# Load sizes at the start, one routing pass and item 0's loads rearranged in a fused attention and mixture-of-experts kernel

## The chip, the cores and the metric

The kernel runs on one core of one Trainium2 chip. The metric is the device time of one execution in microseconds (us), from three runs. "Within 0.2%" means within 1.8 us of the time before.

## The reference

Two stages follow each other; the second takes the first one's output as 14592 tokens of 256 channels.

```python
# q, k, v: (4, 3648, 256)
qn = q / (norm(q, axis=1) + 1e-06)
kn = k / (norm(k, axis=1) + 1e-06)
s = kn.transpose(0, 2, 1) @ qn / tau          # (4, 256, 256)
a = softmax(s)
x = (v @ a).reshape(14592, 256)

# 4 groups of 4 experts; each token takes the best group, then its best expert
g_idx = argmax(x @ w_group);  g_w = softmax weight of that group
e_idx = argmax(x @ w_expert[g_idx]);  e_w = softmax weight of that expert
out = g_w * e_w * (relu(x @ w1[g, e]) @ w2[g, e])   # w1: 256x1024, w2: 1024x256
```

## The kernel before, in words

**Precision.** Most matmuls are made of three fast ones: an operand is split into a high part (a copy on ScalarE, ACT) and a low part (a subtraction on VectorE, DVE), and high by high, high by low and low by high are summed in PSUM on TensorE (PE). A few are left as plain float32; the trace records each of those twice.

**Scores.** q and k of a batch come in eight units of four row groups each (`GJ` = 4; the last of a batch is small); unit `u` is one tile `qkraw` of 128 x 2 x 4 x 256, loaded by `s_load(u)` on SyncE's queue (SP). `LOADS` = 4 units are issued ahead, in five buffers. For unit 0 the loads come in three pairs (row group 0; 1; 2 and 3), for unit 1 in two pairs (0 and 1; 2 and 3), and from unit 2 on one pair, q then k. Each partition's run in memory is 1 KB per row group. `s_split(u)` splits row group 3 (in later units others too) and squares the unit on ACT for the norms, `s_mm(u)` does the matmuls (L240): groups 0 to 2 of the first units are plain, 3 is split. Fourteen `wake` matmuls run before the first load is there.

**Rows of x.** `x_load(u)` brings v, `x_tr(u)` transposes it on PE into two PSUM buffers `vtr` (one per half of the channels) and splits it: `vth` on ACT (L326), `vtl` on DVE (L327). `x_mm(u)` (L349) multiplies by the softmax matrix, which has the routing logits folded in as 20 more columns, and calls `hooks[k]` behind the row groups that they name. With `TM` = 30 the loop `for t in range(TM, len(xs_at))` lays down the order of every engine by hand; `k` counts its turns, and k = 0 is unit 20 of x. `adv(n)` runs n steps of the generators in `rgens`, in their order.

**Routing.** `routing(b, j0, j1)` picks group and expert for the rows of a range in eight steps, nearly all on DVE: steps 1 to 3 pick, 4 counts within a partition, 5 sends the counts to PE and computes the weights, 6 adds the carried counts (L437 to L441), 7 makes the slots `si` (L444, L446), 8 puts the row groups into `pend`. `pre_gen` follows it for the table of the first four items (L558 on, `tb_pre`). Batch 2 has the ranges 0 to 8, 8 to 20 and 20 to 29; `PRE` = (2, 20) ends the rows that the first items are drawn from.

**Scatters.** `scatter(n)` writes each row group of a range to its slots in HBM (`x_sorted`) by an indirect DMA on GpSimd (POOL, L473); behind each stands a `pause()`, a fill of 128x256 zeros (L163).

**Experts.** Items of 512 rows of one expert follow each other. `fetch_w` and `fetch_x` put their loads on SP: for item 0, at k = 8, w1 (1 MB), then its rows (which wait until every scatter up to `PRE` has landed), then w2 in two halves. `split_w` and `split_x` make the high and low parts, `ffn1` (L995 to L1005) and `ffn2` (L1036, L1037, L1045) the two products, `send` scatters the output. Leftover rows go in pieces of 32, four at once on four columns of the array ("quads", `q_ffn1` L1155); `q_xT` turns their rows by 32x64 transposes on DVE (L1140), 16 of them per quad in two lots. They stand behind `split_w` of the next item in the loop over (item, f).

The change touches `s_load` (L186), `scatter` (L483), `fetch_w` and `fetch_x` (L724 to L751), `hooks` (L933), the turn k = 8 (L966), and the place of `q_xT` (L1362).

Of the kernel before, what the change touches and what calls it, by code (L numbers as in the profile page):

```python
# [17 lines left out]
P = 128  # L18
B, NT, C = 4, 3648, 256
N = B * NT  # L20
E = 16
FF = 1024
# [3 lines left out]
GPB = 8  # L26
# [4 lines left out]
RW = 272  # L31
# [19 lines left out]
PRE = (2, 20)  # L51
# [14 lines left out]
def attention_moe(ctx: ExitStack, tc, q, k, v, tau, w_group, w_expert, w1, w2, out):  # L66
# [94 lines left out]
    def pause():  # L161

        POOL.memset(zero[:, 0:256], 0.0)  # L163
# [18 lines left out]
    def s_load(u):  # L182
        rows, nj = rows_of(u % GPB)
        raw = spool.tile([P, 2, GJ, C], F32, tag="raw", name="qkraw", bufs=LOADS + 1)

        for j0, j1 in (((0, 1), (1, 2), (2, nj)), ((0, 2), (2, nj)))[u] if u < 2 else ((0, nj),):  # L186
            for i, src in ((0, q), (1, k)):
                SP.dma_start(raw[:rows, i, j0:j1, :], tiles_of(src, u // GPB, u % GPB)[:, j0:j1, :])
        su[u] = dict(raw=raw)
# [269 lines left out]
    def scatter(n, wait=0):  # L459
        for _ in range(n):  # L460
            if not pend or pend[0][1] + wait > now[0]:
                break
            (b, j0), _, j, si = pend.pop(0)
            g, t = divmod(j0 + j, GJ)
            rows, nj = rows_of(g)
            xs = rows_at[b, g]
            if t == 0:
                tok = xs[:, 0:nj, C].bitcast(I32)
                if g < NG:
                    POOL.iota(tok, pattern=[[-1, GJ]], base=NOID - b * NT - g * GJ, channel_multiplier=-J)  # L470
                else:
                    POOL.iota(tok, pattern=[[0, 1]], base=NOID - b * NT - J * P, channel_multiplier=-1)
            ins = POOL.indirect_dma_start(  # L473
                out=xs_d, out_offset=bass.IndirectOffsetOnAxis(ap=si[:rows, j:j + 1], axis=0),
                in_=xs[:rows, t, 0:RW].bitcast(I32), in_offset=None, bounds_check=NSLOT - 1, oob_is_err=False)
            if not before((b, j0)):
                for o in early:
                    tc.declare_no_dep(ins.ins, o, reason="the first items' slots have been filled")
                late.append(ins.ins)
            for o in scatters:  # L480
                tc.declare_no_dep(ins.ins, o, reason="every token has a slot of its own")
            scatters.append(ins.ins)
            pause()  # L483


    def table_steps(items, cnt, start, held, stride, name):
# [233 lines left out]
    def raw_tile(of=3):  # L720
        raw_n.append(0)
        return wp.tile([P, 2048], F32, tag=f"wraw{len(raw_n) % of}", name="wraw", bufs=1)

    def fetch_w(d, tb, i, which):  # L724
        e = SP.value_load(tb[0][0:1, i, 0:1], min_val=0, max_val=E - 1)
        src, n = (w1e, 2) if which == "w1" else (w2e, 8)
        if d is items[KPRE] and which == "w1":
            raw_n.append(0)
        d[which + "r"] = t = raw_tile(3 if any(d is o for o in items[0:KPRE]) else 2).rearrange("p (c f) -> p c f", c=n)
        for c in range(2) if d is items[0] and n == 8 else ():  # L730
            h = slice(c * n // 2, (c + 1) * n // 2)
            SP.dma_start(t[:, h, :], src[ds(e, 1), c * FF // 2:(c + 1) * FF // 2, :].rearrange("o (c p) f -> p (o c) f", p=P))
        if d is not items[0] or n == 2:
            SP.dma_start(t, src[ds(e, 1), :, :].rearrange("o (c p) f -> p (o c) f", p=P))

    def fetch_x(d, tb, i):

        if d is items[0]:
            d["xg"] = raw_tile()[:, 0:4 * RW].rearrange("p (t w) -> p t w", t=4)
        else:  # L740
            d["xg"] = ring(4, RW, name="xg")
        d["nv"] = tb[1][:, i:i + 1]
        if tb is not tb_pre:
            gather(d["xg"].rearrange("p t w -> p (t w)"), tb[2][:, i:i + 1], 4)
            pause()
            return
        s = SP.value_load(tb[0][0:1, i, 1:2], min_val=0, max_val=DUMMY)
        ins = SP.dma_start(d["xg"].bitcast(I32), xs_d[ds(s, BIG), :].rearrange("(p t) w -> p t w", t=4))
        early.append(ins.ins)
        for o in late:  # L750
            tc.declare_no_dep(ins.ins, o, reason="the first items' slots have been filled")  # L751
# [176 lines left out]
    def where(i):  # L928
# [4 lines left out]
    hooks = {  # L933
        0: {1: [sft()], 2: [sft()]},
        1: {0: [adv()], 1: [sft(), adv()], 2: [sft(2), adv()]},
        2: {0: [sft(), adv()], 1: [sft(), lambda: x_tr(US - GPB)], 2: [adv()], 3: [adv()]},
        3: {0: [adv(2)]},
        4: {0: [adv()], 1: [adv()]},
        5: {0: [adv()], 1: [adv()]},
        6: {0: [adv()], 1: [adv()]},  # L940
        7: {0: [adv()], 1: [adv()]},
# [5 lines left out]
    for t in range(TM, len(xs_at)):  # L947
        x = xs_at[t]
        k = t - TM
        now[0] = t  # L950
        if k == 0:
            soft(2)
        if k == 1:
            sp_.close()
            wp = ctx.enter_context(tc.tile_pool(name="wp", bufs=4))
            vx = vx_.enter_context(tc.tile_pool(name="vx", bufs=VX))
            x_load(x + 2)
            x_load(x + 3, vx)
        if k >= 1 and x + 4 < UX:
            x_load(x + 4, vx if x + 4 == UX - 4 else None)  # L960
        if x + 1 < UX and x + 1 != US - GPB:
            x_tr(x + 1, vx if x + 2 == US - GPB else None)
        if k == 0:
            s_mm(US - 2)
            s_mm(US - 1)
        if k == 8:  # L966
            fetch_w(items[0], tb_pre, 0, "w1")
            fetch_x(items[0], tb_pre, 0)
            fetch_w(items[0], tb_pre, 0, "w2")
        if k == 10:  # L970
            vx_.close()
            wb = ctx.enter_context(tc.tile_pool(name="wb", bufs=4))
        if x == UX - 1:
            fetch_x(items[1], tb_pre, 1)
            fetch_w(items[1], tb_pre, 1, "w1")
            split_x(items[0])
            split_w(0, "w2", 0)
        x_mm(x, hooks[k])
        scatter(NJ)
        queue(x)  # L980
# [161 lines left out]
    def q_xT(q, a):  # L1142
        q_turn(qs["xT"][q % 2], qs["xg"][q % 2][:, a * C // 4:(a + 1) * C // 4].rearrange("p (k c) -> p c k", c=2), a)
# [179 lines left out]
    for n in range(len(seq) + lag):  # L1323
# [3 lines left out]
        if n < len(seq):  # L1327
            i, f = seq[n]
            j, jn = host(i), host(i + 1)
            if f == 3:  # L1330
                if KPRE < i + 2 < NBIG:
                    fetch_x(*where(i + 2))
            if jn is not None and f == 5 and i + 2 < NBIG:
                fetch_big(i + 2, "w1")
            for s_, p_ in plan.get((j, f), ()):
                q_weights(s_, p_)
            if f == 7 and KPRE < i + 2 < NBIG:
                quads_of(items[i + 2])
            if j is not None and f == 1 and i + 1 < NBIG:
                fetch_big(i + 1, "w2")  # L1340
            if first(j) is not None and f == 1:
                q = first(j)
                tokens(qs["ids"][q % 2], qs["xg"][q % 2][:, C:C + 1], slotq, tb_pc[1][:, q:q + 1])
            if i == NBIG - 1 and f == 4:
                POOL.drain()
                ns = nc.values_load(nsub[0:1, 0:1], min_val=0, max_val=NSUB)
                tc.mark_branch_hint_location("subs", engines=[ET.PE, ET.Pool, ET.DVE, ET.Activation, ET.SP])
            if first(jn) is not None and f == 1:
                q_rows(first(jn))
            ffn1(items[i], f)  # L1350
            for h in side.get(n, ((), ()))[0]:
                h()
            if KPRE < i + 1 < NBIG:
                if f in (0, 2):
                    split_w(i + 1, "w1", f // 2)
                if f == 3:
                    turn_x(items[i + 1])
                if f == 4:
                    split_x(items[i + 1])
                if f in (5, 6):  # L1360
                    split_w(i + 1, "w2", f - 5)
            for q, a in ((jn, 0),) if f == 7 else ((j, 2),) if f == 0 else ():  # L1362
                if first(q) is not None:
                    q_xT(first(q), a)
                    q_xT(first(q), a + 1)
            if j is not None:
                s_ = stage(j)
                for second, q, hf in q_stage(s_) if s_ is not None else ():
                    if f == 2:
                        (q_ffn2 if second else q_ffn1)(s_, q, hf)  # L1370
                    if 3 <= f < 7 and not second:
                        q_hT(q, hf, f - 3)
                    if f == 3 and second and hf:
                        q_put(q)
# [115 lines left out]
```

## Time and profile before

| | us |
|---|---|
| median of 3 runs | 909.39 |
| the 3 runs | 909.39, 910.15, 909.3 |
| the profiled execution, its own time | 908.52 |
| span of its trace | 906.7 |
| PE busy | 898.0 (99%) |
| DVE busy | 715.2 (79%) |
| ACT busy | 495.1 (55%) |
| POOL busy | 394.1 (43%) |

A trace row gives start and length in us, engine, source line, operation, output<-inputs, shapes and count; in brackets stands how long the engine was idle before it and what ended that. Rows of the same instruction that follow each other are merged (x12). Matmuls are pipelined: a matmul's listed length is longer than its turn, and from start to start is what counts.

### The profile page before, as it was taken

How to read it: one execution, taken by the hardware profiler on the slowest of the kernel's cores; microseconds unless marked ns; L12 is line 12 of the kernel's file. 1: busy time of each engine (PE TensorE's matmuls, PEld its weight loads, DVE VectorE, ACT ScalarE, POOL GpSimd, SP SyncE). 2: the span in 40 equal slices, each digit the busy share in tenths (PEclk: the TensorE clock that was granted, in tenths of full speed). 3: DMA queues.
4: the chain of work that ended last, by engine and by line, in shares of the span. 5: the costliest groups of instructions: out<-in, count | busy, mean ns of one | idle time of the engine just before them, and what ended most of it. 6: DMA issues, size and time to landing. Idle time of an engine off the chain costs nothing. (4 is left out here: it accounts for less than half of the span.)

```text
span 906.7 us, 16702 instructions
## 1 busy us (share of the span) xinstructions
PE 898.0 (99%) x5454; PEld 767.9 (85%) x5454; DVE 715.2 (79%) x1533; ACT 495.1 (55%) x832; POOL 394.1 (43%) x569
## 2 busy tenths in 40 slices
PE   9999999999999999999999999999999999999997
PEld 7899999999899987878787887878787878787887
DVE  6898999977999968888898767787677858786852
ACT  6788788776554444544455444444444444444432
POOL 0001887888588783423332233333433334223223
PEclk9999999999999999999999999999999999999999
DMA  8984868465954476566777778777776667777751
GB/s 301 352 313 163 304 238 298 152 206 183 310 186 167 157 229 213 202 214 232 251 250 251 247 255 260 255 252 238 250 227 227 227 221 236 241 237 255 243 168 39
DMA packets 156075, 209.68 MB, mean 231 GB/s; under 512 B 63025, under 2 KB 115602, under 8 KB 155984
## 3 DMA queue, kind: packets, MB, share of 16 engines
q1 hardware_dynamic: 140928, 164.03, 55.4%
q0 software_dynamic: 15056, 44.54, 13.1%
q8 instruction: 44, 0.72, 0.3%
q14 instruction: 47, 0.39, 0.1%
HBM read 166.14 MB, written 31.17 MB: 218 GB/s over the span
## 5 line engine op out<-in xcount | busy, mean ns | idle before, releaser
L1014 ACT ACTIVATE hh<-hmm 128x512 fp32r<-128x512 f32 (+1 forms) x222 | 131.9, 595 | 337.2 <-PE hmm L1005 279.1
L1005 PE MATMUL hmm<-xth,ww 128*128 128x512 f32 (+1 forms) x888 | 312.3, 392 | 0.0
L1066 POOL DMA_INDIRECT out<-ys,ids x112 | 125.4, 1120 | 356.2 <-DVE ys L1055 331.9
L1036 PE MATMUL wacc<-ww,hh 128*128 128x512 f32 (+1 forms) x736 | 265.6, 394 | 0.0
L1015 DVE SCALAR_TENSOR_TENSOR hl<-hmm,hh 128x512 fp32r<-128x512 f32 (+1 forms) x222 | 151.1, 683 | 110.3 <-ACT hh L1014 91.2
L1037 PE MATMUL wacc<-ww,hl 128*128 128x256 f32 (+1 forms) x736 | 206.2, 280 | 0.0
L1005 PEld LDWEIGHTS hmm<-xth,ww 128*128 128x128 f32 x888 | 166.7, 188 | 36.1
L1005 PE MATMUL hmm<-xtl,ww 128*128 128x512 f32 (+1 forms) x444 | 174.0, 392 | 0.0
L1036 PEld LDWEIGHTS wacc<-ww,hh 128*128 128x128 f32 (+1 forms) x736 | 137.5, 187 | 36.5 <-issue 4.1
L473 POOL DMA_INDIRECT x_sorted<-xs,si x112 | 132.3, 1182 | 58.8 <-issue 26.0
L792 DVE TENSOR_TENSOR ww<-wraw,ww 128x1024 fp32r<-128x1024 f32 x112 | 136.7, 1221 | 19.5 <-ACT ww L791 15.6
L1037 PEld LDWEIGHTS wacc<-ww,hl 128*128 128x128 f32 (+1 forms) x736 | 138.7, 188 | 7.0
L791 ACT ACTIVATE ww<-wraw 128x1024 fp32r<-128x1024 f32 x112 | 117.9, 1053 | 3.9 <-DMA wraw<-in_moe_w 3.8
L1005 PEld LDWEIGHTS hmm<-xtl,ww 128*128 128x128 f32 x444 | 83.8, 189 | 9.6
L163 POOL MEMSET zero<- 128x256 f32 x260 | 87.1, 335 | 0.1
L349 PE MATMUL xmm<-ahi,vth 128*128 128x276 f32 (+1 forms) x232 | 69.1, 302 | 0.6 <-ACT xs L352 0.5
L240 PE MATMUL sacc<-qkraw 128*128 128x256 f32 (+1 forms) x276 | 68.3, 389 | 0.7 <-DMA qkraw<-in_k 0.7
L349 PE MATMUL xmm<-alo,vth 128*128 128x276 f32 (+1 forms) x232 | 67.3, 291 | 0.0
L349 PE MATMUL xmm<-ahi,vtl 128*128 128x276 f32 (+1 forms) x232 | 67.2, 291 | 0.0
L224 DVE TENSOR_TENSOR sqa<-sqa,sq 128x1024 f32<-128x1024 f32 (+3 forms) x46 | 59.7, 1308 | 5.5 <-ACT sq L211 3.9
L240 PEld LDWEIGHTS sacc<-qkraw 128*128 128x128 f32 (+1 forms) x276 | 50.7, 194 | 7.7 <-issue 1.8
L352 ACT ACTIVATE xs<-xmm 128x276 f32<-128x276 f32 x112 | 42.3, 410 | 23.3 <-PE xmm L349 11.8
(316 smaller groups left out, 1438.9 us busy)
## 6 DMA issues: line engine op xcount, KB each, us to landing
wraw<-in_moe_w SPq DMA_DIRECT2D x55, 1024.0 KB
qr<-in_moe_w SPq DMA_DIRECT2D x44, 512.0 KB
vr<-in_v SPq DMA_DIRECT2D x28, 512.0 KB
qkraw<-in_q SPq DMA_DIRECT2D x26, 512.0 KB
qkraw<-in_k SPq DMA_DIRECT2D x26, 512.0 KB
xq<-xg SPq DMA_DIRECT2D x368, 32.0 KB
qraw<-in_moe_w SPq DMA_DIRECT2D x22, 512.0 KB
qw<-in_moe_w SPq DMA_DIRECT2D x22, 512.0 KB
```

The costliest lines, as they stand in the source:

```text
L163: POOL.memset(zero[:, 0:256], 0.0)
L240: PE.matmul(d["acc"][:, c, :], kt[:rows, 1, cs], qt[:rows, 0, :], start=d.pop("first", True) and c == 0, stop=(g == NG), skip_group_check= ...
L349: PE.matmul(mm[:rows, :NE], vt[:, c, j * P:j * P + rows], at[:, c, :], start=(n == 0), stop=(n == 5))
L473: ins = POOL.indirect_dma_start(out=xs_d, out_offset=bass.IndirectOffsetOnAxis(ap=si[:rows, j:j + 1], axis=0), in_=xs[:rows, t, 0:RW].bitc ...
L791: ACT.activation(h, r, AF.Copy)
L792: DVE.tensor_tensor(l, r, h, ALU.subtract)
L1005: PE.matmul(mm, wt[:, c, fs], xt[:, c, :], start=(n == 0), stop=(n == 5))
L1014: ACT.activation(hh, mm, AF.Relu)
L1015: d["hl"] = DVE.scalar_tensor_tensor(hl, mm, 0.0, hh, ALU.max, ALU.subtract)
L1036: PE.matmul(d["acc"][t][:m].rearrange("p c n -> p (c n)"), hh[:, tsl], d["w2w"][:, f, :], start=(f == 0), stop=(f == 7), skip_group_check= ...
L1037: PE.matmul(d["acc"][t][:m, 0, :], hl[:, tsl], d["w2h"][:, f, :], start=False, stop=(f == 7), skip_group_check=True)
L1066: ins = POOL.indirect_dma_start(out=out, out_offset=bass.IndirectOffsetOnAxis(ap=d["ids"][:lanes(d), t:t + 1], axis=0), in_=d["ys"][:lanes ...
```

## The change

- Unit 0 comes in two pairs (row group 0; 1 to 3), unit 1 in one pair: ten loads for units 0 to 3 where there were fourteen.
- The fills behind the 12 scatters of batch 2's range 8 to 20 are left out.
- Steps 6, 7 and 8 of that range's routing move from k = 2 (behind row group 3) and k = 3 to k = 4, behind row group 0: they now follow the `vtl` subtractions of `x_tr` at k = 4 (unit 25) on DVE, and stand right ahead of the first step of the table.
- Item 0's first half of w2 is issued ahead of its rows, and waits until w1 has landed; the second half stays behind the rows.
- A quad's transposes stand ahead of the next item's `split_w` in the same f (at f = 0; at f = 7 nothing stands between the two places).

```diff
-        for j0, j1 in (((0, 1), (1, 2), (2, nj)), ((0, 2), (2, nj)))[u] if u < 2 else ((0, nj),):
+        for j0, j1 in ((0, 1), (1, nj)) if u == 0 else ((0, nj),):
...
-            pause()
+            if not (2, 8) <= (b, j0) < PRE:
+                pause()
...
     def fetch_w(d, tb, i, which):
-        e = SP.value_load(tb[0][0:1, i, 0:1], min_val=0, max_val=E - 1)
+        if d is not items[0] or which == "w1":
+            e = d["e"] = SP.value_load(tb[0][0:1, i, 0:1], min_val=0, max_val=E - 1)
...
+    def fetch_half(d, c):
+
+        h = slice(c * 4, (c + 1) * 4)
+        ins = SP.dma_start(d["w2r"][:, h, :], w2e[ds(d["e"], 1), c * FF // 2:(c + 1) * FF // 2, :].rearrange("o (c p) f -> p (o c) f", p=P))
+        if c == 0:
+            tc.add_manual_dep(ins.ins, d["w1i"].ins.name,
+                              mybir.DependencyInfo(mybir.DependencyClass.Sync, mybir.DependencyReason.DATA),
+                              reason="one matrix behind the other")
...
-        2: {0: [sft(), adv()], 1: [sft(), lambda: x_tr(US - GPB)], 2: [adv()], 3: [adv()]},
-        3: {0: [adv(2)]},
-        4: {0: [adv()], 1: [adv()]},
+        2: {0: [sft(), adv()], 1: [sft(), lambda: x_tr(US - GPB)], 2: [adv()]},
+        3: {},
+        4: {0: [adv(4)], 1: [adv()]},
...
             fetch_w(items[0], tb_pre, 0, "w1")
+            items[0]["xg"] = raw_tile()[:, 0:4 * RW].rearrange("p (t w) -> p t w", t=4)
+            fetch_w(items[0], tb_pre, 0, "w2")
+            fetch_half(items[0], 0)
             fetch_x(items[0], tb_pre, 0)
-            fetch_w(items[0], tb_pre, 0, "w2")
+            fetch_half(items[0], 1)
...
+            for q, a in ((jn, 0),) if f == 7 else ((j, 2),) if f == 0 else ():
+                if first(q) is not None:
+                    q_xT(first(q), a)
+                    q_xT(first(q), a + 1)
             if KPRE < i + 1 < NBIG:
                 if f in (0, 2):
                     split_w(i + 1, "w1", f // 2)
...
-            for q, a in ((jn, 0),) if f == 7 else ((j, 2),) if f == 0 else ():
-                if first(q) is not None:
-                    q_xT(first(q), a)
-                    q_xT(first(q), a + 1)
```

## Rows read from the trace of the kernel before

**Rows 1.** Page, busy time of each engine.

```profile
PE 898.0 (99%) x5454; PEld 767.9 (85%) x5454; DVE 715.2 (79%) x1533; ACT 495.1 (55%) x832; POOL 394.1 (43%) x569
```

**Rows 2.** Waits of PE over the span: us in total, times, longest.

```profile
PE sacc L240 <- DMA qkraw<-in_k: 0.7, 2, 0.4
PE vtr L325 <- DVE vtl L327: 0.6, 1, 0.6
```

**Rows 3.** Timeline of the first 21 us, PE and ACT.

```profile
4.37 4.21 PE L240 MATMUL sacc<-qkraw 128*128 128x256 f32 x12
...
7.25 0.63 ACT L202 ACTIVATE qkhi<-qkraw 128x512 fp32r<-128x512 f32 x1 [4.85 <-DMA qkraw<-in_k]
...
8.23 0.47 PE L240 MATMUL sacc<-qkhi 128*128 128x256 f32 x1
...
9.95 2.83 PE L240 MATMUL sacc<-qkraw 128*128 128x256 f32 x12 [0.43 <-DMA qkraw<-in_k]
...
12.43 0.47 PE L240 MATMUL sacc<-qkhi 128*128 128x256 f32 x1
...
13.80 2.83 PE L240 MATMUL sacc<-qkraw 128*128 128x256 f32 x12 [0.32 <-DMA qkraw<-in_k]
...
17.30 2.75 PE L240 MATMUL sacc<-qkraw 128*128 128x256 f32 x12
...
20.61 2.75 PE L240 MATMUL sacc<-qkraw 128*128 128x256 f32 x12
```

**Rows 4.** L240 in one stretch: length, PE, PEld, PEclk, DMA share, GB/s.

```profile
4.36:7.30 2.94, 2.93 (x7) 2.37 (x8) 1.00 0.88 284
```

**Rows 5.** Two stretches, every engine; last DMA share and GB/s.

```profile
2.00:10.00 8.00, 7.57 (x32) 6.42 (x30) 3.10 (x27) 2.82 (x4) 0.32 (x2) 1.00 0.91 273
10.00:16.00 6.00, 5.68 (x28) 4.97 (x29) 3.11 (x4) 4.66 (x4) 0.00 (x0) 1.00 1.02 415
```

**Rows 6.** Timeline of PE around k = 4 and k = 5.

```profile
206.76 1.25 PE L325 MATMUL vtr<-ident,vr 128*128 128x128 f32 x8 [0.59 <-DVE vtl L327]
207.77 0.38 PE L349 MATMUL xmm<-ahi,vth 128*128 128x276 f32 x1
...
210.92 1.04 PE L325 MATMUL vtr<-ident,vr 128*128 128x128 f32 x8
211.71 0.37 PE L349 MATMUL xmm<-ahi,vth 128*128 128x276 f32 x1
```

**Rows 7.** Timeline of DVE in the same stretch.

```profile
204.15 0.14 DVE L437 TENSOR_TENSOR bs<-pp,carry 128x16 f32<-128x16 f32 x1
...
205.94 0.24 DVE L446 CAST si<-sf 128x12 int32<-128x12 f32 x1
206.03 1.28 DVE L327 TENSOR_TENSOR vtl<-vtr,vth 128x512 fp32r<-128x512 f32 x2
...
209.75 1.28 DVE L327 TENSOR_TENSOR vtl<-vtr,vth 128x512 fp32r<-128x512 f32 x2
```

**Rows 8.** Timeline of POOL: first and last of the 12 scatters; a later one.

```profile
206.96 0.99 POOL L473 DMA_INDIRECT x_sorted<-xs,si  x1 [0.72 <-POOL xs L470]
...
223.71 0.97 POOL L473 DMA_INDIRECT x_sorted<-xs,si  x1 [0.17 <-issue]
...
251.58 2.01 POOL L473 DMA_INDIRECT x_sorted<-xs,si  x1 [0.17 <-issue]
```

**Rows 9.** Timeline of SP: item 0's w1 and its rows.

```profile
216.59 0.04 SPq L734 DMA_DIRECT2D wraw<-in_moe_w  x1
226.43 0.35 SPq L748 DMA_DIRECT2D wraw<-x_sorted  x1
```

**Rows 10.** Timeline of PE: item 0's rows turned.

```profile
230.41 1.11 PE L837 MATMUL xtr<-ident,wraw 128*128 128x128 f32 x8
```

**Rows 11.** Timeline of DVE and PE at a quad, one of eleven stages.

```profile
397.57 2.05 DVE L1140 STREAM_TRANSPOSE qxT<-qxg 32x64 f32<-32x64 f32 x8
400.21 0.62 PE L1155 MATMUL qmm<-qraw,qxT 128*32 128x512 f32 x1
```

More of the change, by code (lines that the diff above doesn't have):

```diff
@@ L729, in fetch_w @@
         d[which + "r"] = t = raw_tile(3 if any(d is o for o in items[0:KPRE]) else 2).rearrange("p (c f) -> p c f", c=n)
-        for c in range(2) if d is items[0] and n == 8 else ():
-            h = slice(c * n // 2, (c + 1) * n // 2)
-            SP.dma_start(t[:, h, :], src[ds(e, 1), c * FF // 2:(c + 1) * FF // 2, :].rearrange("o (c p) f -> p (o c) f", p=P))
         if d is not items[0] or n == 2:
-            SP.dma_start(t, src[ds(e, 1), :, :].rearrange("o (c p) f -> p (o c) f", p=P))
+            d[which + "i"] = SP.dma_start(t, src[ds(e, 1), :, :].rearrange("o (c p) f -> p (o c) f", p=P))
+    def fetch_half(d, c):
[5 more added lines that the diff above has]
+                              reason="one matrix behind the other")
     def fetch_x(d, tb, i):
-        if d is items[0]:
-            d["xg"] = raw_tile()[:, 0:4 * RW].rearrange("p (t w) -> p t w", t=4)
-        else:
+        if d is not items[0]:
             d["xg"] = ring(4, RW, name="xg")
```

## The prediction, made before the changed kernel was run

> **What bounds the kernel now.** The page's busy table comes first: PE is busy 99% of the span, DVE 79%, ACT 55%, POOL 43% [rows 1]. An edit that takes work from another engine is therefore worth only the time that PE stands still, or runs slowly, because of it. The list of PE's waits says how much that is: apart from its start, PE waited 0.7 us for first loads of q and k and 0.6 us for `vtl` on DVE [rows 2]; nothing of the expert stage, three quarters of the span, is in the list above half a microsecond. So the question is how much of some 2 us can be won, and whether the change opens a new wait. A measurement of this kernel can tell about 0.2%, 1.8 us, from no change.
>
> The timeline of the start shows three losses [rows 3]. A unit without a wait takes 3.31 us (17.30 to 20.61). Unit 1 starts at 9.95, after unit 0's split matmuls began at 8.23; from 9.95 to its own split matmuls (12.43) unit 1 takes 2.48, so a unit's split part is 3.31 - 2.48 = 0.83, and unit 1 could have begun at about 9.1. It stood about 0.85 us, in part for the load and in part for unit 0's late split: ACT got the last quarter of unit 0 only at 7.25. Unit 1 to unit 2 takes 3.85, 0.54 too many, again for a load. Unit 2 to unit 3 takes 3.50, 0.19 too many. The sum is near 1.6 us.
>
> The third loss is pace: between 4.36 and 7.30 PE got through 7 plain matmul records in 2.94 us, 0.42 each [rows 4], against 2.48 / 12 = 0.21 later. The clock column says 1.00 there, but half the pace is what 1.2 of 2.4 GHz would give, after PE had run the wake matmuls.
>
> **Longer first runs.** Bytes to landing: unit 0 is 1.05 MB. Its first pair (0.26 MB) is there by 4.37 [rows 3], before and after. The other 0.79 MB now come as 3 KB runs, and none can be used before all are in. The bounds of the rate are 273 GB/s for 2 to 10 us, where runs are 1 and 2 KB, and 415 GB/s for 10 to 16 us, where they are 4 KB [rows 5]. So unit 0 is whole between 4.2 + 1.9 = 6.1 and 4.2 + 2.9 = 7.1; I take 6.4, as 3 KB is nearer to 4 KB (before: 7.25). PE ends row group 0 (4 records) at 4.37 + 4 x 0.42 = 6.05, so there is a new pause of 0.35 us in the place where 1 KB of row group 1 used to be enough. Then two records at 0.42 and six at 0.21 end at 8.5, the split part at 9.35. Unit 1 (1.05 MB, 4 KB runs) is whole at 6.4 + 2.5 = 8.9 with 415 GB/s, 10.2 with 273; by 4 KB runs I take 8.9, so PE goes on at 9.35, not 9.95. Unit 2 starts at 9.35 + 3.31 = 12.66, not 13.80, and its load is in by 11.5: **-1.1 us**, which I round down to -1.0 because the last piece of each unit came late by more than the mean rate gives. With the slow ends (7.1, 10.9 for unit 1) unit 2 starts at 14.2: +0.4. Without the pause and with no wait at all it is the 1.6 above. The four loads less on SP count for nothing by themselves; SP is not what the loads wait for.
>
> The Trainium skill ("DMA: Bandwidth & Descriptors", Specifications) puts the smallest transfer for line rate at 512 B. By that rule 1 KB runs were already at full rate, and this part would bring nothing. The trace disagrees so far as two stretches can show it: DMA engines were 0.91 and 1.02 busy at 273 and 415 GB/s [rows 5]; but the first stretch also holds each queue's beginning.
>
> **Low halves ahead of counts.** At k = 5 PE waits for `vtl` of unit 25: transposes 206.76, next matmuls 207.77, where a turn without a wait takes 0.79 (210.92 to 211.71) [rows 6]. With 0.59 before it the loss is some 0.8 us. On DVE, steps 6 and 7 (204.15 to 206.03) stood ahead of that `vtl` [rows 7]. Now `vtl` goes first, at 204.15, and is done by 205.43: this stall goes. But what is late next? Steps 6, 7, 8 and the table's first two steps still stand ahead of the next `vtl`, and DVE has no idle time between 204.15 and 209.75; so that `vtl` starts at 209.75 as before, and its first half (0.64) is ready at 210.4. PE would want its buffer 0.8 earlier than before, at 210.1, and gets the first at 210.45, the second at 211.05. The matmuls behind it start at about 211.5 instead of 211.71. Of 0.8 us **-0.2** is left; the bounds are 0 and -0.8.
>
> **No fills behind 12 scatters.** The slots `si` come from step 7, done at 206.18 before. Behind the `vtl` they are done 1.28 later, so the first scatter moves from 206.96 to 208.2. The 12 stand 1.52 apart (16.75 / 11) [rows 8]; without the fill 0.97 + 0.17 = 1.14, with two index fills some 1.18. The last starts at 208.2 + 11 x 1.18 = 221.2, not 223.71. Rows of item 0 are issued 2.72 behind the last scatter [rows 8, 9]: 223.9, not 226.43. PE turns them at 230.41 without a wait [rows 10], so 3.98 us after issue is enough, and they gain 2.4 us of slack that PE has no use for: 0. No trace row shows a scatter of rows without a fill behind it; the bounds are 1.14 and, for the crowded ones, 2.01 + 0.17 = 2.18 apart [rows 8], and I take the first because the DMA is no more crowded here than in most of the 12.
>
> **Item 0's w2.** SP now waits for w1 before half of w2 and, behind that, the rows. w1 is issued at 216.59 [rows 9] and needs 2.5 to 3.8 us at the rates above, so it is in by about 221, before the rows can be asked for (223.9). The half's 0.5 MB (1.3 to 1.9 us) are through by then. Nobody on PE waits for w2 [rows 2]: 0. If scatters were quicker still, the rows would wait behind w1, with 2.4 us to spare.
>
> **Quads.** The second lot of transposes ends at 399.62, 0.59 before the quad's first matmul [rows 11]; ahead of `split_w` it ends over a microsecond sooner, and the weights are needed an item later. PE has no wait there in any stage [rows 2]: 0.
>
> **Sum.** -1.0 - 0.2 = -1.2 us against the profiled execution's 908.52 (span 906.7 and 1.8 around it), 907.3. That execution is 0.87 under the median of 909.39, so the median comes to 908.2. Whatever PE wins early it keeps, as no later wait is on anything but work that PE sets.
>
> **Rivals.**
> 1. *Both stalls go and no new one comes*: 3 KB runs land by 6.1 and DVE's chain is quicker; -1.6 - 0.8 = 907.0. For it: the 415 GB/s. Against: DVE without idle time [rows 7]. Chance 0.20.
> 2. *The start only moves its wait*: the rate stays at 273 GB/s, PE pauses at row group 1 and wins nothing at unit 1; 909.39 - 0.2 = 909.2. For it: the slow stretch is the beginning of all loads, whatever their runs. Against: the rate is 415 as soon as the runs are 4 KB [rows 5]. Chance 0.16. The rule that the Trainium skill ("DMA: Bandwidth & Descriptors", Specifications) gives for 512 B leads here too.
> 3. *The pause keeps the slow pace*: PE stands at 6.05, and the step up that came at 7.3 comes later. If it lasts through unit 0, eight records at 0.42 from 6.4 and a split part of 1.66 end at 11.4; unit 2 starts at 14.7, +0.9 - 0.2, 910.1. Chance 0.10. The skill's page "TensorE: Matmul & The Clock Gate" (Part 1) says that the slow state is the default and activity releases it, which would make such a pause count; no row here has a pause at that place.
> 4. *Slower*: scatters without fills run into each other. Rows are then late on PE from the point where 208.2 + 11 s + 2.72 + 3.98 passes 230.2, s = 1.39 a scatter; at s = 1.66 the loss outweighs the win by 1.8 us, and at 2.18 it is 8.7, 916.9. For it: 2.01 occurs with a fill behind each [rows 8]. Against: the first and the last of the 12 take 0.99 and 0.97. Chance 0.07.
>
> **Numbers.** The forecast, with its own range of 907.6 to 909.0, has 0.47. The range reaches from rival 1's end to rival 3: 906.9 to 910.2, leaving out rival 4 and the tails. Faster by over 0.2% needs 907.57 or less, rival 1 and a little of the forecast: 0.22. Slower by over 0.2% is most of rival 4 and a longer rival 3: 0.08. Within: 0.70.
>
> **What would show it.** Right: PE idle for a load at about 6 us once and no more at units 1 and 2; unit 2's plain matmuls begin near 12.7; `vtl` of unit 25 starts near 204 on an unshifted scale, and PE's wait for `vtl` comes a turn later, smaller; scatters 1.15 to 1.2 apart; half of w2 issued before the rows; PE's waits in sum near 1 us. Wrong: plain matmuls at 0.42 beyond 8 us, PE idle before item 0's transposes, or scatters over 1.4 us apart.

## The result, and the profile after

The changed kernel takes **919.12 us** (median of 5, 918.29 to 920.77), the kernel before 909.39 on the same chip (median of 5, 908.89 to 910.15): ratio 1.011 [1.0098, 1.0121], 9.7 us slower. The forecast was 908.2 and its range ended at 910.2. The profiled execution took 920.65, with a span of 918.9.

The page first; its row answers to [rows 1].

```profile
PE 903.7 (98%) x5454; PEld 771.0 (84%) x5454; DVE 713.6 (78%) x1533; ACT 495.6 (54%) x832; POOL 390.2 (42%) x557
```

POOL is 3.9 us less busy, 12 instructions fewer: the fills are gone. The span is 12.2 longer and PE only 5.7 busier, so it also stands still more. Milestones of the two traces place the loss. At unit 4 (the last row below against 20.61 [rows 3]) the changed kernel is 0.83 late; at the turn of `vtl` it is 0.24 late (its matmuls at 211.95 against 211.71 [rows 6]); item 0's transposes, 230.41 in [rows 10], now begin at 241.56, **11.15 late**; the last matmul of the span is 12.2 late. Nearly all goes within 30 us, just where the 12 scatters without fills stand.

The start, timeline of PE, the plain matmuls of units 0 to 4 (they answer to [rows 3]):

```profile
4.38 1.91 PE L240 MATMUL sacc<-qkraw 128*128 128x256 f32 x4
7.43 3.55 PE L240 MATMUL sacc<-qkraw 128*128 128x256 f32 x8 [1.14 <-DMA qkraw<-in_k]
...
11.54 2.75 PE L240 MATMUL sacc<-qkraw 128*128 128x256 f32 x12
...
14.84 2.75 PE L240 MATMUL sacc<-qkraw 128*128 128x256 f32 x12
...
18.14 2.75 PE L240 MATMUL sacc<-qkraw 128*128 128x256 f32 x12
...
21.44 0.81 PE L240 MATMUL sacc<-qkraw 128*128 128x256 f32 x3
```

The pause stands at row group 1, and behind it eight matmuls run at half pace (from 7.43 to the next form at 10.62 that is 0.40 each), though the clock column says 1.00 (L240 in that stretch; columns as in [rows 4]):

```profile
7.43:10.62 3.19, 3.19 (x8) 2.53 (x9) 1.00 1.01 408
```

Then no unit waits: 3.30 from start to start, where before units 1 and 2 began late for loads.

The waits of PE from 200 to 245 us:

```profile
PE xmm L349 <- issue: 5.1, 7, 1.5
PE vtr L325 <- DVE vtl L327: 1.3, 1, 1.3
```

"issue" means that nothing in the trace tells what PE waited for. The stretches around it (PE, PEld, DVE, ACT, POOL busy, then granted clock, DMA share, GB/s):

```profile
212.00:217.00 5.00, 5.00 (x43) 5.00 (x41) 3.54 (x19) 1.23 (x3) 3.87 (x5) 1.00 0.33 114
217.00:222.00 5.00, 2.33 (x10) 1.49 (x10) 0.00 (x0) 0.80 (x2) 4.04 (x5) 1.00 0.89 305
222.00:227.00 5.00, 1.97 (x7) 1.56 (x6) 0.00 (x0) 1.23 (x4) 2.15 (x4) 0.53 0.68 206
227.00:232.00 5.00, 4.19 (x19) 4.19 (x20) 4.69 (x12) 3.76 (x11) 0.00 (x0) 0.50 0.76 245
...
222.28:232.52 10.24, 6.51 (x28) 6.11 (x28) 5.17 (x13) 5.00 (x13) 2.11 (x3) 0.50 0.73 232
```

DVE has nothing at all from 217 to 227 and ACT hardly anything: they starve along with PE. PE stood for 2.67 + 3.03 + 0.81 = 6.5 us, and after it had stood, the granted clock fell to 0.50, the lower of its two levels (1.2 of 2.4 GHz), for 10.24 us; the 6.51 us that PE was busy there are worth half, 3.3. Together 9.8 of some 11. In the kernel before, PE was busy throughout from 217 to 232, at a clock of 1.00; its rows from 222 on:

```profile
222.00:227.00 5.00, 5.00 (x43) 4.79 (x41) 2.79 (x9) 3.22 (x9) 2.85 (x5) 1.00 0.23 84
227.00:232.00 5.00, 5.00 (x41) 4.92 (x40) 4.57 (x18) 4.52 (x12) 1.28 (x1) 1.00 0.84 258
```

The Trainium skill ("TensorE: Matmul & The Clock Gate", HAM oscillation — how this bites in real kernels) describes waits for data behind which PE falls back to its slow clock; the row for 222.28 to 232.52 agrees that the clock falls behind a standstill, though here PE stood in pieces of 1.5 us at most and none was a wait for a load.

Why ACT had nothing to do shows in its timeline, beside the last matmuls of row groups 0 and 1 of the same unit on PE:

```profile
212.67 0.29 PE L349 MATMUL xmm<-ahi,vtl 128*128 128x276 f32 x1
...
213.43 0.29 PE L349 MATMUL xmm<-ahi,vtl 128*128 128x276 f32 x1
```

```profile
213.61 0.40 ACT L352 ACTIVATE xs<-xmm 128x276 f32<-128x276 f32 x1 [0.78 <-PE xmm L349]
219.25 0.40 ACT L352 ACTIVATE xs<-xmm 128x276 f32<-128x276 f32 x1 [5.24 <-remote]
221.41 0.40 ACT L352 ACTIVATE xs<-xmm 128x276 f32<-128x276 f32 x1 [1.75 <-remote]
225.69 0.40 ACT L352 ACTIVATE xs<-xmm 128x276 f32<-128x276 f32 x1 [3.88 <-remote]
```

Row group 0 was copied 0.94 after its last matmul began (212.67 to 213.61), row group 1 **5.82** after (213.43 to 219.25), with ACT idle and waiting all that time for a signal of PE. I call this time the *lag*. With ACT free and nothing in the way it is 0.33; in the kernel before it reaches 2.33 in this stretch, in the changed one 10.8. It grows from row group to row group (0.94, 5.82, then 7.2 and 10.8), and from 217 us on PE stands too. Its seven pauses marked "issue" all lie inside a row group, between matmuls that go into the same PSUM buffer, so they are not waits for a buffer that ACT has still to empty; what holds PE there the trace does not tell.

The trace also records when an engine's signals arrive. From 205 to 232 us every recorded signal of ACT, DVE and POOL stands within 0.1 us of the end of an instruction that gives it. ACT's last three copies wait for a signal of PE and for nothing else, and the ones that release them, at 219.23, 221.38 and 225.67, stand 2.36, 1.75 and 3.27 us behind the last matmul that gives one (hence "remote": the rows name no engine). So it is the signal that is late, and not ACT.

The scatters (first, second, last of the 12) and SP's issues for item 0 (w1, half of w2, the rows; they answer to [rows 8, 9]):

```profile
209.25 0.99 POOL L473 DMA_INDIRECT x_sorted<-xs,si  x1 [2.19 <-issue]
210.55 0.97 POOL L473 DMA_INDIRECT x_sorted<-xs,si  x1 [0.30 <-issue]
...
223.62 0.97 POOL L473 DMA_INDIRECT x_sorted<-xs,si  x1 [0.30 <-issue]
```

```profile
216.53 0.54 SPq L733 DMA_DIRECT2D wraw<-in_moe_w  x1
222.00 0.39 SPq L738 DMA_DIRECT2D wraw<-in_moe_w  x1
227.09 0.35 SPq L754 DMA_DIRECT2D wraw<-x_sorted  x1
```

They are 1.27 apart, 1.31 with the index fills (14.37 / 11), where they were 1.52 [rows 8]. The scatters themselves are as long as before; what shrank is the time between two of them, from 0.53 to 0.33 on average. The rows are there long before PE turns them.

### The profile page after: what moved, and what is told of

Read it like the earlier page. It is cut to its first block, busy times and chain, and to the rows that moved or that the text cites. A ratio compares the mean times of both kernels' runs of the same rounds, so it can differ in the third digit from the quotient of the medians.

```text
span 918.9 us, 16679 instructions
## 1 busy us (share of the span) xinstructions
PE 903.7 (98%) x5454; PEld 771.0 (84%) x5454; DVE 713.6 (78%) x1533; ACT 495.6 (54%) x832; POOL 390.2 (42%) x557
## 5 line engine op out<-in xcount | busy, mean ns | idle before, releaser
L163 POOL MEMSET zero<- 128x256 f32 x248 | 83.1, 335 | 0.1
L240 PE MATMUL sacc<-qkraw 128*128 128x256 f32 (+1 forms) x276 | 69.4, 393 | 1.1 <-DMA qkraw<-in_k 1.1
L240 PEld LDWEIGHTS sacc<-qkraw 128*128 128x128 f32 (+1 forms) x276 | 51.1, 196 | 8.5 <-issue 2.5
```

What stands on the lines that cost most here:

```text
L240: PE.matmul(d["acc"][:, c, :], kt[:rows, 1, cs], qt[:rows, 0, :], start=d.pop("first", True) and c == 0, stop=(g == NG), skip_group_check= ...
```

## Experiments

Kernels of one group ran on one chip beside the kernel before: its median was 909.15 in the first group, 914.03 in the second (another chip, 911.44 to 915.82), 909.70 in the third. Ratios are against those. "a" kernels start from the changed kernel, "b" kernels from the one before; F in the first group's expectations is the theory that the missing fills make the loss, C that the pause at the start does.

**First group: which part is it?** The changed kernel with the 12 fills back:

```diff
-            if not (2, 8) <= (b, j0) < PRE:
-                pause()
+            pause()
```

> The changed kernel with the 12 fills put back, all else as changed. Theory F (without fills the scatters stand 1.27 us apart instead of 1.52, and PE, which waits for nothing that the trace names from 217 to 226 us, is held up by them): the gaps of PE with no releaser vanish, the granted clock stays at its upper level from 222 to 232 us, and the time comes back to 909.39 + 0.9 for the start - 0.7 for the routing steps = 909.6, between 908.8 and 910.6. Rival W (the half of w2 that waits on SP for w1, and its load, hold PE up): the fills change nothing, 918 to 920.

908.77, 0.9996 [0.9984, 1.0009]. The kernel before with only the fills left out:

```diff
-            pause()
+            if not (2, 8) <= (b, j0) < PRE:
+                pause()
```

> The kernel before with only the 12 fills left out. Theory F: PE stands still without a named releaser while these scatters run, 916 to 919. Rival W: nothing on PE changes, 909.2 to 909.6. If the fills need the scatters to lie later (with the routing steps moved), something between.

918.78, 1.0112 [1.0091, 1.0132]. Then the first loads: the kernel before with only the longer first runs, and the changed one with the first loads of before (the same diff the other way).

```diff
-        for j0, j1 in (((0, 1), (1, 2), (2, nj)), ((0, 2), (2, nj)))[u] if u < 2 else ((0, nj),):
+        for j0, j1 in ((0, 1), (1, nj)) if u == 0 else ((0, nj),):
```

> The kernel before with only the longer first loads. Theory C (the pause of 1.1 us at row group 1 puts off the step of the granted clock from 7.3 to 10.7 us): unit 2 starts at 14.8 instead of 13.8, and 0.8 to 1.0 us are still lost at 20 us; 910.1 to 910.5. Rival (as the prediction had it): unit 2 starts near 12.7, 908.4.

> The changed kernel with the first loads as before. Theory C with F: the stall of PE near 217 us stays, 0.9 us less at the start, 917.4 to 918.8. Rival: if the stall hangs on where PE is when the scatters run, 909 to 915.

908.73, 0.9996 [0.9982, 1.001], and 919.44, 1.0118 [1.0097, 1.014]. **The 12 fills are the whole loss**, with or without the other parts; the start is worth nothing that these runs can tell, and C falls as the cause: its kernel was not slower. With the fills back PE's waits in the same stretch are:

```profile
PE xtr L842 <- DMA wraw<-x_sorted: 1.1, 1, 1.1
```

No standstill, but a small new wait for rows, to which I come back. In the kernel of before without fills it can be told whose signals are late. ACT's high halves `vth`, then DVE's low halves `vtl` of the same two buffers:

```profile
217.30 0.60 ACT L326 ACTIVATE vth<-vtr 128x512 fp32r<-128x512 f32 x1 [0.73 <-PE xmm L349]
220.13 0.60 ACT L326 ACTIVATE vth<-vtr 128x512 fp32r<-128x512 f32 x1 [2.23 <-PE vtr L325]
```

```profile
217.93 0.69 DVE L327 TENSOR_TENSOR vtl<-vtr,vth 128x512 fp32r<-128x512 f32 x1 [5.12 <-issue]
220.76 0.69 DVE L327 TENSOR_TENSOR vtl<-vtr,vth 128x512 fp32r<-128x512 f32 x1 [2.14 <-issue]
```

DVE starts 0.03 us after ACT ends (217.90, 220.73), though it had been idle for 5.12: ACT's signal is prompt. ACT itself starts over 5 us after the transposes, which PE had behind it at 212. So it is **PE's signals**, and not ACT's, that come late while scatters follow closely. PE's waits in this kernel, from 200 to 245 us:

```profile
PE vtr L325 <- DVE vtl L327: 2.8, 2, 2.2
PE vtr L325 <- issue: 1.7, 1, 1.7
PE xmm L349 <- issue: 1.4, 4, 0.4
```

The Trainium skill ("SBUF — State Buffer", Who interferes with whom) says that PE and ACT never wait on anyone, and that only VectorE and GpSimd share a port. As a rule on memory ports no run here speaks against it; as a rule on what can stall PE it does not hold in this stretch: nothing but GpSimd's instructions was changed in this kernel, and PE stood for 2.8 + 1.7 + 1.4 = 5.9 us.

**Second group: what must stand between two scatters?** Fills of one column instead of 256; a fill behind every second scatter; none behind the first six:

```diff
+            if (2, 8) <= (b, j0) < PRE:
+                POOL.memset(zero[:, 0:1], 0.0)
+            else:
+                pause()
```

> The kernel before, with the fills behind batch 2's row groups 8 to 19 cut from 128x256 to 128x1: an instruction on POOL stands between two scatters as before, but the pace rises from 1.66 us to an estimated 1.3 to 1.4 (without any fill it was 1.27). Theory T (a signal of PE gets out only in the time between two scatters, so the time counts): lags of ACT's copies behind PE of some us, PE stands still after 215, time 914 to 919. Rival I (any instruction between two scatters is enough): lags as in the kernel before, at most 2.4 us, time 908.5 to 910.

920.48, 1.0068 [1.0047, 1.009]. The scatters stand 1.32 apart (14.48 / 11); the lag climbs through 3.2, 6.8 and 9.6 to 12.4, PE waits 3.9 with "issue" and 4.6 for `vtl`, the clock falls. An instruction in between is not enough: rival I falls.

```diff
-            pause()
+            if not (2, 8) <= (b, j0) < PRE or j % 2:
+                pause()
```

> The kernel before, with a fill only behind every second of the same 12 scatters. Theory T: half of the room for signals, the lag of ACT's copies reaches 3 to 6 us, PE stands still for at most 2 us and its clock may hold: 909.5 to 914. Rival I: each gap with a fill empties what has gathered, lags at most 2.5 us and 908.5 to 910. If the loss were fixed by the scatters' number alone it would be 918.8 again.

920.47, 1.0057 [1.0034, 1.0081]; 1.41 apart, lags up to 9.3. More than I expected of theory T.

```diff
+            if not (2, 8) <= (b, j0) < PRE or j >= 6:
+                pause()
```

> The kernel before, without fills behind the first six of the same 12 scatters, with them behind the last six. PE's standstill began 7.6 to 8.4 us after the first scatter without a fill; six of them take 7.6. Theory T: the lag grows to 4 to 6 us by the sixth and shrinks again behind the fills, PE loses 0 to 3 us and keeps its clock: 908.8 to 912. If one long stretch is not needed and six are enough for the whole loss: 917 to 919.

920.11, 1.0057 [1.0035, 1.0079]: a miss, it lost as much as the others. ACT's timeline shows why.

```profile
216.54 0.40 ACT L352 ACTIVATE xs<-xmm 128x276 f32<-128x276 f32 x1 [3.90 <-PE xmm L349]
...
222.35 0.40 ACT L352 ACTIVATE xs<-xmm 128x276 f32<-128x276 f32 x1 [2.34 <-PE vtr L325]
...
225.21 0.98 ACT L352 ACTIVATE xs<-xmm 128x276 f32<-128x276 f32 x3 [2.45 <-PE xmm L349]
```

The lag was 4.74 at 216.54, when the sixth scatter was through, and did not shrink behind the fills that followed: 8.92, then 11.00. In this run one fill behind each scatter did not work off a backlog. This chip may bear less in any case: the next kernel, with every fill of batch 2 in place, has lags up to 5.5 there, where the kernel before had 2.33 in its trace, and loses 4.4 us between 199 and 223 us against that trace. That may be why the kernel before takes 914 on this chip; its trace on it was not taken.

The same twelve-fold omission in batch 0:

```diff
+            if not (0, 8) <= (b, j0 + j) < (0, 20):
+                pause()
```

> The kernel before, without fills behind batch 0's row groups 8 to 19 instead (they are scattered from about 107 to 127 us, while PE does scores and transposes; all fills of batch 2 stay). Theory T says that the place does not matter: the copies lag behind PE by more and more over 15 us, PE stands still in the span's second fifth, and the time is 914 to 919, the clock down for some 10 us. Rival L (what is late is only what batch 2's second range holds: counts, low halves, the first items' rows): nothing happens at 107 to 127, 908.5 to 910.

916.75, 1.0033 [1.0009, 1.0058]: 2.7 us, where the other three cost 6.1 to 6.5 on this chip. In the stretch concerned the lag stays at 2.6 or less and the clock at 1.00; PE loses 1.8 us there (against the trace of the kernel before it is 0.44 early at 98 us and 1.35 late at 117). Neither expectation holds; POOL's timeline shows what differs from batch 2.

```profile
103.10 0.99 POOL L473 DMA_INDIRECT x_sorted<-xs,si  x1 [0.28 <-POOL xs L470]
104.40 0.97 POOL L473 DMA_INDIRECT x_sorted<-xs,si  x1 [0.30 <-issue]
...
111.81 1.92 POOL L473 DMA_INDIRECT x_sorted<-xs,si  x1 [0.30 <-issue]
114.04 1.44 POOL L473 DMA_INDIRECT x_sorted<-xs,si  x1 [0.31 <-issue]
...
119.81 0.98 POOL L473 DMA_INDIRECT x_sorted<-xs,si  x1 [0.31 <-issue]
```

Here scatters are stretched by something of their own and stand 1.52 apart on average (103.10 to 119.81, 11 steps), as far as filled ones do in batch 2; the time between two of them is as short as without fills elsewhere, 0.33 on average. So the distance from start to start goes with the small lag, but T as it was worded, with signals that get out only between two scatters, does not fit. It was read afterwards, and the engines do other work there: this run does not decide.

**Third group: more room, and a better version.** Two fills behind each of the 12 scatters:

```diff
             pause()
+            if (2, 8) <= (b, j0) < PRE:
+                pause()
```

> The kernel before with two fills instead of one behind each of the same 12 scatters, estimated 1.9 us from start to start. Theory T (PE's signals need the time between scatters): ACT's copies behind PE by at most 1.3 us in this stretch, where one fill left up to 2.3 and none 11.7; PE does not stand still for its signals and keeps its clock. What it costs is the rows: the last scatter lands some 4.5 us later, item 0's first transpose waits for them by name and begins at 233 to 236, ratio 1.003 to 1.006. If lags come from something else in this stretch (the tables, the loads), they stay at 1.8 to 2.4.

The lags are as T says: ACT waits for each product and has it at once.

```profile
215.75 0.40 ACT L352 ACTIVATE xs<-xmm 128x276 f32<-128x276 f32 x1 [0.32 <-PE xmm L349]
216.53 0.40 ACT L352 ACTIVATE xs<-xmm 128x276 f32<-128x276 f32 x1 [0.37 <-PE xmm L349]
217.29 0.40 ACT L352 ACTIVATE xs<-xmm 128x276 f32<-128x276 f32 x1 [0.36 <-PE xmm L349]
```

From 206 to 227 no lag is over 0.38. That settles by dose that the room counts: on the chips of the first and third group and in the first pair of kernels the lag reaches 10.8 to 11.7 with the scatters 1.31 apart (no fill), 1.2 to 2.6 with 1.51 to 1.52 (one), and with 2.13 (two) it is gone. Whether the distance or the time between two is what counts these kernels cannot tell, as the scatters are equally long in them. A rival falls with it: if ACT waited for a buffer `xs` until a scatter had emptied it, later scatters would make the lag longer, and here they end 4.9 us later than in the kernel before. POOL's busy time is not what counts, as the same stretch of three kernels shows (the kernel before, the one without fills, the one with two each; columns as above):

```profile
207.00:222.00 15.00, 15.00 (x122) 14.82 (x121) 12.46 (x44) 10.72 (x27) 13.22 (x22) 1.00 0.50 167
```

```profile
207.00:222.00 15.00, 10.22 (x71) 9.05 (x72) 7.18 (x30) 5.12 (x13) 11.37 (x14) 0.88 0.33 119
```

```profile
207.00:222.00 15.00, 15.00 (x124) 15.00 (x123) 11.42 (x41) 10.73 (x28) 11.48 (x23) 1.00 0.44 144
```

POOL is busy for 11.37 and 11.48 in the last two, and PE does 10.22 in one, 15.00 in the other. Nor is it the traffic as a whole: 144 and 167 GB/s where PE is undisturbed, 119 where it stands. But the kernel is slow for its other end: 918.21, **1.011 [1.0092, 1.0128]**, the price I put at half that.

```profile
236.91 1.31 PE L839 MATMUL xtr<-ident,wraw 128*128 128x128 f32 x5 [8.08 <-DMA wraw<-x_sorted]
```

PE waits 8.08 us for the rows by name, and then works at a granted clock of 0.68 from 235 to 245; the lower level was missing in my price. So one fill stands between two cliffs, of 9.6 us on one side (918.78 against 909.15) and 8.5 on the other (918.21 against 909.70).

The wait for rows came back with the fills. Is it w2's first half, now ahead of them? The changed kernel with the 12 fills back, and w2 moved as well:

```diff
-            if not (2, 8) <= (b, j0) < PRE:
-                pause()
+            pause()
...
+            fetch_x(items[0], tb_pre, 0)
             fetch_w(items[0], tb_pre, 0, "w2")
             fetch_half(items[0], 0)
-            fetch_x(items[0], tb_pre, 0)
             fetch_half(items[0], 1)
```

> The changed kernel with the 12 fills back and item 0's rows ahead of w2 again: first loads, low halves and quads remain. With the fills alone put back, PE waited 1.1 us at 229 to 230 for the rows behind w2's first half. If that order made the wait, it is gone and item 0's first transpose stands at 228.8 to 229.8: ratio 0.997 to 0.9995. If the rows are late anyway (the scatters end no sooner than before), the wait stays and the ratio is 0.9995 to 1.0005.

909.27, 1.0001 [0.9992, 1.001]; PE still waits 1.18, so the order of w2 is not the cause. The kernel before with only the steps of the second range moved shows what is:

```diff
-        2: {0: [sft(), adv()], 1: [sft(), lambda: x_tr(US - GPB)], 2: [adv()], 3: [adv()]},
-        3: {0: [adv(2)]},
-        4: {0: [adv()], 1: [adv()]},
+        2: {0: [sft(), adv()], 1: [sft(), lambda: x_tr(US - GPB)], 2: [adv()]},
+        3: {},
+        4: {0: [adv(4)], 1: [adv()]},
```

> The kernel before with only the steps of batch 2's second range moved (v's low halves ahead of the counts). By the prediction the wait for the low halves moves on by one turn and 0.2 us are gained, ratio 0.9998; by the trace of the changed kernel (its offset fell by 0.7 us between 203 and 215) 0.9992. Both within what is told apart from no change; 1.0005 or more would speak against both.

910.68, 1.001 [1.0, 1.002]. Its scatters and its rows:

```profile
208.26 0.99 POOL L473 DMA_INDIRECT x_sorted<-xs,si  x1 [2.19 <-issue]
...
224.93 0.97 POOL L473 DMA_INDIRECT x_sorted<-xs,si  x1 [0.16 <-issue]
```

```profile
231.40 1.20 PE L837 MATMUL xtr<-ident,wraw 128*128 128x128 f32 x8 [1.22 <-DMA wraw<-x_sorted]
```

The first scatter moves from 206.96 [rows 8] to 208.26, since the slots now come behind the low halves, the last from 223.71 to 224.93, and PE waits 1.22 for the rows. Its interval begins at 1.0, so it is no better than the kernel before, against my expectation: what the low halves win, the rows take back.

A few scatters without fills at the very end should then be allowed (the changed kernel, fills behind the first nine):

```diff
-            if not (2, 8) <= (b, j0) < PRE:
+            if not (2, 8) <= (b, j0) < PRE or j < 9:
                 pause()
```

> The changed kernel with fills behind the first nine of the 12 scatters and none behind the last three, w2's first half still ahead of the rows. A standstill of PE needs 7 to 8 us of scatters without a fill, by the traces so far; three take 3.8. Theory T: the lag of ACT's copies grows by about 1 to 2 us at the end, PE does not stop, the rows land about 0.8 us sooner and the wait for them is 0 to 0.6 us instead of 1.1: ratio 0.998 to 1.000. If a few at the end are enough to set PE back, 1.003 to 1.010.

**908.38, 0.9987 [0.9978, 0.9996]**, the only one of the twelve whose interval lies below 1, though by less than the 0.2% set at the outset, and among twelve intervals one so close to 1 can be chance. The lag ends at 2.45, PE does not stand for signals, and the wait for rows is gone; in its place stands 0.90 for split weights (`ww` on DVE).

## Why the prediction was wrong

*What bounds the kernel*: held. Some 2 us were to be won; the question was what the change opens.

*No fills, 0*: this is **the step that failed**. It took the fills for a delay of the scatters, found that their going gives "2.4 us of slack that PE has no use for", and bounded the unknown by the scatters' own pace. The pace was near enough (1.31 against 1.18). What no bound covered is that the room between scatters is used by somebody else: PE's signals. The term, put at 0, was +9.6 us (918.78 against 909.15 with the fills alone left out). Two rows of the timeline of ACT in the kernel before carried the hint and were not taken up:

```profile
218.22 0.40 ACT L352 ACTIVATE xs<-xmm 128x276 f32<-128x276 f32 x1 [0.95 <-PE xmm L349]
...
223.44 0.99 ACT L352 ACTIVATE xs<-xmm 128x276 f32<-128x276 f32 x3 [1.48 <-PE vtr L325]
```

ACT idles for 0.95 and 1.48 us for products that PE had behind it (lags 1.83 and 2.33, where 0.33 is the rule). An operation that computes nothing was taken out without asking what its duration holds off.

*Rival 4* had the right place and sign, and a price of 8.7 at its far end, but another mechanism: rows late by scatters running into each other. The scatters stayed at 0.97 and the rows were there before PE turned them.

*Longer first runs, -1.0*: the step held in most executions. The pause, put at 0.35, was 0.29 and 0.41 in two of the five traces with the new loads and 0.88 to 1.19 in three, but unit 2 started at 12.63, 12.65, 12.76 and 13.17 in four of the five (12.66 predicted), and between 12.46 and 13.80, in the middle 13.41, in the nine without. The fifth is the changed kernel's own profile, 14.84: there rival 3 came true (14.7). The step to full pace came at a time of its own in each execution, with either loads, so this rival is a chance of every run, not a cost of the change. Rivals 1 and 2 differ from the forecast in time by less than these runs tell, but rival 2's condition, a rate that stays at 273 GB/s, does not hold: from 4 to 7 us all five traces with the new loads show 380 to 404 GB/s, the nine with the old ones 259 to 304. So the more and shorter runs of before were not at full rate. In the times the gain is not seen: 0.9996 [0.9982, 1.001]. In that kernel's trace item 0 begins 1.24 sooner (229.17), but the stretch from there to the last matmul is 1.18 longer; over the traces that stretch ranges from 670.3 to 674.0 whichever parts a kernel has, and hides an effect of this size.

*Low halves, -0.2*: the stall moved on by a turn, as said, and the gain was nearer 0.7 (0.92 late at 203.77, 0.24 at 211.95). The working even had the price, "1.28 later" for the first scatter (1.30 measured), but spent it against the scatters' new pace. With the old pace the rows are 1.2 late. "Whatever PE wins early it keeps" fails with it: item 0's rows are a wait that POOL's chain sets, and it was about to become the bound.

*Item 0's w2, 0* and *quads, 0*: held as far as the traces tell; no run has either by itself. The wait for rows was 1.1 with w2's half ahead, 1.2 without. From item 0's transposes to the last matmul it took 670.3 to 671.7 in the five traces with the new quads, 670.5 to 671.8 in four with the old ones on the same chips (the kernel with two fills, whose clock was low there, left aside).

## What to carry to other kernels

An instruction that produces nothing is part of the schedule: before it goes, look at who uses the time that it takes, above all at late signals on the engines around it (an engine idle for microseconds behind a producer that the trace shows as done). A margin between two chains should be looked up from both sides: here one fill more behind each scatter costs 8.5 us and one less 9.6, since PE's standstill is followed by its lower clock, and only the last three could go. Put single edits beside the bundle: by themselves the first loads and the moved routing steps shifted the median by 1.0 us or less, the fills by 9.6.

## What the runs showed of the hardware

- While indirect DMAs on POOL follow each other at 1.27 to 1.4 us in batch 2, PE's signals reach ACT up to 12 us late; ACT's reach DVE in 0.03 us all the while. Two fills in between (2.13 apart) bring PE's back to 0.33. In batch 0, scatters without fills that stood 1.52 apart went with 2.6 at most. By which path a scatter holds the signals up was not tried.
- PE's standstills (6.5 us in pieces, 8.1 in one) were followed by the lower granted clock: 0.50 over 10.24 us in the changed kernel, 0.68 in the mean of 235 to 245 with two fills. In the changed kernel that added half of the wait again.
- The pace of plain matmuls at the start doubles at a moment of its own, by 4.3 us in one execution and near 10.7 in another, while the clock column shows 1.00 in the stretches read (4.36 to 7.30 before, 7.43 to 10.62 after).
- The first loads move 380 to 404 GB/s from 4 to 7 us in fewer loads with runs of 3 and 4 KB, 259 to 304 in more loads with runs of 1 and 2 KB.
